# A decode block with its backward pass on one core: the last second-pass heads two by two, with 2 MiB gradient tiles

## The chip, the core and the metric

The kernel runs on one core of a Trainium2 chip. Its engines are TensorE (PE, with its weight loads shown as PEld), VectorE (DVE), ScalarE (ACT), GpSimd (POOL) and SyncE (SP, which here only issues transfers); 16 DMA engines move data between DRAM and the on-chip memory. The metric is the device time of one execution in microseconds, lower is better.

## The reference

One transformer decode block (two sequences, one new token each) and its vector-Jacobian product. What matters here is attention over a long cache and the gradients of that cache, which are as large as the cache itself.

```python
B, Sq, D = 2, 1, 640
Hq, Hkv, Sk, Dh = 32, 32, 4096, 128
...
q = (x @ wq).reshape(B, Sq, Hq, Dh)   # transposed to b h q d
scores = einsum("bhqd,bhkd->bhqk", q, k) * (Dh ** -0.5)
p = softmax(scores)
o = einsum("bhqk,bhkd->bhqd", p, v)
...
h  = x + A(layernorm(x), k_cache, v_cache, wq, wo)
h2 = h + B(layernorm(h), w1, w2)       # B: relu MLP, 640 -> 1728 -> 640
...
out, vjp = jax.vjp(f, x, k_cache, v_cache, wq, wo, w1, w2)
grads = vjp(grad_out)
```

For each of the 64 heads (2 sequences x 32) the gradients of the cache are outer products: gV = p times go (the gradient that reaches this head's output), and gK = ds times q, with ds = p * (V go - p.(V go)). Each is 4096 x 128 in bf16, 1 MiB. So 64 MiB of K and 64 MiB of V are read, 52 MiB of V are read a second time, and 128 MiB of gradients are written, beside some MiB of weights and weight gradients.

## The kernel before

The program records every engine's instructions in an order of its own, with generators that are advanced step by step; no scheduler moves them. A first pass (`p1_iter`) goes over all heads, reads K and V and makes scores, probabilities and outputs. A second pass (`p2_iter` and `p2_tail`) goes over the heads in the order `turns`, reads V again as tile `Wt` unless it was kept, and makes gV and gK. Between and beside them, background generators make the MLP, the weight gradients (`outer_rows`, tile `ot`, stored from ACT's queue) and the gradient of the input (`gx_gen`, which multiplies rows of wq on DVE, L669).

A head in the second pass lies as 128 partitions x 32 rows of 128, that is 8 KiB in a partition, both in DRAM and on chip (`natural`, L457). One head goes like this:

- POOL copies the head's probabilities twice beside each other (`pp`, L885); for some heads it also makes `pf` (L888).
- PE spreads the head's go and scaled q over all partitions into a PSUM bank (L878); ACT scales them by the head's softmax factor `rt` into `rb` (L883).
- V is transposed in four groups: four PE transposes into one of two PSUM banks (`t_ps`, L442), and an ACT copy out of it (`t_sb`, L447). Eight small matvecs per group (L455) then make `dp` = V go.
- DVE makes gV in two halves as an outer product of `rb` and `pp` (L843). In the last three heads ACT makes 4 of its 32 columns (L910). POOL issues the store (L911).
- In `p2_tail`, which runs inside the next head's steps, DVE makes ds (`gsp`, L854) and gK in two halves (L843), and POOL issues its store (L862).

Loads are issued by SP from one list (`queue`, emptied by `pump`) as long as a free tile of class `ld` is there. Large tiles of 8 KiB per partition are kept in classes: `ld` (loads), `g` (gradients), `f` (weight gradients), `q` (rows of wq, w2 and gq). `share` says how many tiles a class should own, and `give` hands a returned tile to a class that lacks one. When all of go is known (near the start of the last 20 heads) the space of wo is released, and a pool `big3` adds six tiles there: one `ld`, two `g`, three `q`. A tile is reused only after the transfer or the instructions that still use it have finished.

The main loop goes through `plan`, pairs of a first-pass and a second-pass index. In its late part it steps the second pass, `pump` and three background queues in turn.

Of the kernel before, what the change touches and what calls it, by code (L numbers as in the profile page):

```python
# [7 lines left out]
FP32 = mybir.dt.float32  # L8
BF16 = mybir.dt.bfloat16
# [6 lines left out]
def kernel(  # L16
# [20 lines left out]
    nc = tc.nc  # L37
# [41 lines left out]


    NBIG = 13
    homes = {"ld": list(range(NBIG)), "g": [], "f": [], "q": []}
    free = {tag: len(v) for tag, v in homes.items()}
    owned = dict(free)
    wanted = {}
# [11 lines left out]

    def goes_to(tag):

        if owned[tag] > wanted.get(tag, len(pools)):  # L100
            for other in homes:
                if owned[other] < wanted.get(other, 0):
                    return other
        return tag
# [329 lines left out]
    def pair_transpose(nat, g, dve=False, busy=0):  # L434
# [12 lines left out]
            nc.scalar.copy(out=t_sb[:], in_=t_ps[:])  # L447
        return t_sb

    def pair_matvec(dst, t_sb, g, vecs):  # L450
        v = t_sb[:].bitcast(BF16).rearrange("p j (k two) -> p j k two", two=2)
        for j in range(GT // 2):
            sc = g * GT + 2 * j
            for par in range(2):
                nc.tensor.matmul(dst[:, sc:sc + 2], lhsT=v[:, j, :, par], rhs=vecs[:, par, :],  # L455
                                 start=(par == 0), stop=(par == 1))
# [4 lines left out]
    def load_tile(what, i, tag):  # L461
        t = take(tag, [128, NSC, 128], what + "t")
        nc.sync.dma_start(out=t[:], in_=natural(A_k_cache if what == "K" else A_v_cache,
                                                *(turns if what == "W" else pairs)[i]))
        (S2 if what == "W" else S1).setdefault(i, {})[what] = t
        (S2 if what == "W" else S1)[i][what + "g"] = tag

    def p1_iter(i, dve_group, busy):

# [378 lines left out]
    def p2_tail(j):  # L848

        p = S2[j]  # L850
        bp, hp = turns[j]
        pair_matvec(p["dp"], p.pop("T3"), 3, gom[:, bp, hp, :, :])
        gsp = small.tile([128, NSC, 2], BF16, tag="gsp", bufs=2, name="gsp")
        nc.vector.scalar_tensor_tensor(  # L854
            out=gsp[:], in0=p["dp"][:, :, None].to_broadcast([128, NSC, 2]), scalar=negdot[:, hp, bp:bp + 1],
            in1=P_bf[:, p_slot[(bp, hp)], :, None].to_broadcast([128, NSC, 2]), op0=ALU.add, op1=ALU.mult)
        yield
        gK = take("g", [128, NSC, 128], "gK")
        outer_half(gK, p["rb"][:, 128:256], gsp, 0)
# [5 lines left out]
        yield  # L865

    NSB = 8

    def p2_iter(j, nsb):

        tail = p2_tail(j - 1) if j - 1 in S2 and "T3" in S2[j - 1] else iter(())
# [251 lines left out]
    while i <= NP1 + 1 or j <= NP1:  # L1123
        ii = i if i <= NP1 + 1 else None
        jj = j if i >= NP1 or (i >= P2_AT and (i - P2_AT) % 2 == 0) else None
        plan.append((ii, jj))
        i += 1
        if jj is not None:
            j += 1


    queue = []
# [3 lines left out]
    for n, (ii, jj) in enumerate(plan):  # L1136
        if ii is not None:
            if ii < NP1:
                queue.append(("K", ii))
        if ii is not None and ii >= 2:  # L1140
            queue.append(("V", ii - 2))
        ahead = plan[n + 1][1] if n + 1 < len(plan) and ii is not None else jj
        if ahead is not None and ahead < NP1 and turns[ahead] not in kept and ("W", ahead) not in queue:
            queue.append(("W", ahead))
        if ii in W_AT:
            queue.append(("w", W_AT.index(ii)))
        if ii in W2_AT:
            queue.append(("w2", W2_AT.index(ii)))
    def pump():
        while queue:  # L1150
            what, k = queue[0]
            if what == "w":
                load_weights(k)
            else:
                tag = "ld"
                if free["ld"] < 1:
                    return
                if what == "w2":
# [24 lines left out]
    for n, (i, j) in enumerate(plan):  # L1183
# [7 lines left out]
        if all_go and not late[0]:  # L1191
            wop.release()
            big3 = tc.alloc_tile_pool(name="big3", bufs=1, side="right")
            for tag in ("ld", "g", "g", "q", "q", "q"):
                more_home(tag, big3)
        late[0] = all_go
        more = int(late[0])
        if fin is not None and not bg2 and not bg3:
            share(ld=8 + 3 * more, g=7 + 3 * more)
        elif fin is not None and j >= H:  # L1200
            held = sum(bh in kept for bh in turns[j + 1:])
            share(ld=5 + held + more, g=5 + 2 * more, f=3, q=2 + 3 * more)
        while g2 is not None:
            p2_step()
        open_tail = [k for k in S2 if "T3" in S2[k]]
        if j is not None:
            if j < NP1:
                bg_until(("go", *turns[j]))
            nsb = 0 if i is not None else NSB if j < H and fin is None else NSB // 2 if j >= NP1 - 3 else 0
            g2 = p2_iter(j, nsb) if j < NP1 else p2_tail(NP1 - 1)  # L1210
# [20 lines left out]
        if i is None:  # L1231
            spread[0] = 2
            at_k[0] = 1
            k = 0
            while g2 is not None:
                p2_step()
                pump()
                slot[0] = int(k in ((1, 3, 5) if j <= H else (1, 4)))
# [69 lines left out]
```

## Time and profile before

| what | value |
|---|---|
| runs | 891.4, 893.67 (median), 894.74 us |
| profiled execution | 892.4 us, its span 890.6 us |
| DMA | 361.84 MB, mean 406 GB/s |
| busy | PE 83%, PEld 70%, DVE 77%, ACT 53%, POOL 23% |
| one gradient product (L843, 128 x 2048) | 1.22 us on DVE, 256 in all |
| gV store, issue to landing | 6.3 us least, 15.1 median, 35.7 most |
| gK store, issue to landing | 9.0 us least, 15.4 median, 35.9 most |
| last gK store issued | 874.91 us |

The page of the profile gives the busy time per engine, the span in 40 slices of 22.3 us with the share of the DMA engines and the rate, the DMA queues with packets and bytes, and the costliest groups of instructions by line. The trace also answers with busy time in any window, with an engine's instructions in order of time, and with who waited for whom. A transfer shows in two places: the instruction that issues it, and the packets on the 16 DMA engines, each of which carries a sixteenth of it.

### The profile page before, as it was taken

The page shows a single profiled execution, that of the slowest core. Times are in us where ns is not written, and L with a number is a line of the kernel's source. Part 1 is how long each engine was busy: PE and PEld are TensorE (multiplying, and loading weights), DVE is VectorE, ACT ScalarE, POOL GpSimd, SP SyncE. Part 2 cuts the span into 40 slices and gives each one's busy share as a digit, 9 for nine tenths or more (in the row PEclk, how much of TensorE's full clock was granted, in tenths as well). Part 3 has the DMA queues.
Part 4 walks back from the last instruction along what each step waited for, and adds up shares of the span by engine and source line. Part 5 has one row for each costly group of instructions (what it writes and reads, how often), then busy time and mean ns, then how long its engine had stood idle before and what let it go on. Part 6 is the DMA issues. An engine that isn't in the chain of part 4 may idle for free. (4 is left out here: it accounts for less than half of the span.)

```text
span 890.6 us, 24645 instructions
## 1 busy us (share of the span) xinstructions
PE 740.5 (83%) x10145; PEld 622.4 (70%) x10145; DVE 687.8 (77%) x1283; ACT 469.7 (53%) x1184; POOL 204.3 (23%) x342
## 2 busy tenths in 40 slices
PE   4999899999999998888888767885888888658871
PEld 4887788888887887777777656764666665536561
DVE  2665779876789897796796888786988467899992
ACT  1344334443455665454547766554567766437751
POOL 1344434342310000000023321121323011111141
PEclk9999989999999999997995555555557765555555
DMA  9999999999889999999999999999999999999995
GB/s 377 419 411 404 409 407 419 410 415 408 350 325 369 422 422 424 422 421 424 422 390 423 420 419 420 419 416 416 391 404 413 424 425 425 424 426 424 423 421 245
DMA packets 56304, 361.84 MB, mean 406 GB/s; under 512 B 5696, under 2 KB 11904, under 8 KB 15488
## 3 DMA queue, kind: packets, MB, share of 16 engines
q1 hardware_dynamic: 34536, 211.13, 58.1%
q0 software_dynamic: 18432, 134.23, 36.2%
q10 hardware_dynamic: 3224, 14.92, 4.1%
q8 instruction: 80, 1.31, 0.6%
q14 instruction: 32, 0.26, 0.1%
HBM read 211.11 MB, written 149.13 MB: 404 GB/s over the span
## 5 line engine op out<-in xcount | busy, mean ns | idle before, releaser
L447 ACT COPY t_sb<-t_ps 128x512 f32<-128x512 f32 x479 | 273.1, 587 | 186.3 <-PE t_ps L442 181.7
L455 PEld LDWEIGHTS <-t_sb 128*128 128x128 bf16 x4096 | 169.9, 103 | 83.7 <-ACT t_sb L447 42.3
L442 PE MATMUL t_ps<-ident_f,Wt 128*128 128x128 f32 x832 | 201.0, 393 | 0.4 <-ACT t_sb L447 0.4
L483 DVE TENSOR_TENSOR pk<-Kt,ep 128x2048 bf16<-128x2048 bf16 x128 | 156.2, 1221 | 44.7 <-ACT ep L534 24.9
L476 PE MATMUL m_ps<-pk,Vt 128*128 128x129 bf16 x2048 | 176.1, 223 | 13.3 <-DMA Vt<-in_A_v_cache_dram 12.6
L843 DVE TENSOR_TENSOR gK<-rb,gsp 128x2048 bf16<-128x2048 bf16 x128 | 153.8, 1226 | 28.0 <-DMA out_dram<-gV 26.2
L843 DVE TENSOR_TENSOR gV<-rb,pp 128x2048 bf16<-128x2048 bf16 (+2 forms) x128 | 147.1, 1172 | 30.8 <-DMA out_dram<-gK 24.0
L442 PEld LDWEIGHTS t_ps<-ident_f,Wt 128*128 128x128 f32 x832 | 140.4, 205 | 31.9 <-issue 25.0
L442 PE MATMUL t_ps<-ident_f,Kt 128*128 128x128 f32 x1024 | 154.7, 287 | 4.6 <-DMA Kt<-in_A_k_cache_dram 4.5
L476 PEld LDWEIGHTS <-Vt 128*128 128x128 bf16 x2048 | 131.0, 99 | 16.9 <-DMA Vt<-in_A_v_cache_dram 14.9
L442 PEld LDWEIGHTS t_ps<-ident_f,Kt 128*128 128x128 f32 x1024 | 117.0, 148 | 6.1 <-issue 3.4
L493 POOL COPY pk<-ep 128x16 bf16<-128x16 bf16 x80 | 83.1, 1041 | 151.3 <-ACT ep L534 112.7
L455 PE MATMUL dp_ps<-gom,t_sb 128*128 128x2 bf16 x2048 | 96.0, 168 | 23.3 <-ACT t_sb L447 22.9
L911 POOL DMA_DIRECT2D out_dram<-gV x64 | 34.3, 536 | 307.8 <-DVE nb L526 114.3
L455 PE MATMUL s_ps<-gom,t_sb 128*128 128x2 bf16 x2048 | 80.2, 164 | 1.2 <-DVE t_sb L445 1.2
L862 POOL DMA_DIRECT2D out_dram<-gK x64 | 34.1, 533 | 202.0 <-DVE gK L843 156.8
L593 ACT CAST MT<-m_ps 128x128 bf16<-128x128 f32 x64 | 17.1, 266 | 116.3 <-PE m_ps L476 116.3
L978 ACT CAST ot<-o_ps 128x512 bf16<-128x512 f32 (+3 forms) x152 | 67.0, 498 | 9.7 <-DMA out_dram<-ot 8.5
L883 ACT ACTIVATE rb<-dp_ps,rt 128x256 bf16<-128x256 f32 x64 | 30.2, 472 | 46.5 <-PE dp_ps L878 44.8
L669 DVE CUSTOM_DVE_ANT_0 rows<-wo_t,rows 128x640 bf16<-128x640 bf16 x64 | 52.3, 817 | 0.4 <-ACT rows L647 0.2
L669 DVE CUSTOM_DVE_ANT_0 rows<-wqs,gqr 128x1024 bf16<-128x1024 bf16 x40 | 48.8, 1219 | 0.2
L669 DVE CUSTOM_DVE_ANT_0 rows<-w_t,rows 128x640 bf16<-128x640 bf16 (+2 forms) x58 | 45.8, 790 | 1.2 <-ACT rows L647 0.5
(194 smaller groups left out, 720.4 us busy)
## 6 DMA issues: line engine op xcount, KB each, us to landing
Kt<-in_A_k_cache_dram SPq DMA_DIRECT2D x64, 1024.0 KB, 16.4
Vt<-in_A_v_cache_dram SPq DMA_DIRECT2D x64, 1024.0 KB, 16.6
out_dram<-gV POOLq DMA_DIRECT2D x64, 1024.0 KB, 15.1
out_dram<-gK POOLq DMA_DIRECT2D x64, 1024.0 KB, 15.4
Wt<-in_A_v_cache_dram SPq DMA_DIRECT2D x52, 1024.0 KB, 11.8
out_dram<-ot ACTq DMA_DIRECT2D x6, 960.0 KB, 12.4
wq_t<-in_A_wq_dram SPq DMA_DIRECT2D x5, 1024.0 KB, 11.0
wqs<-in_A_wq_dram SPq DMA_DIRECT2D x5, 1024.0 KB, 16.1
```

The costliest lines, as they stand in the source:

```text
L442: nc.tensor.transpose(t_ps[:, j, :], natf[:, 2 * cc:2 * cc + 2, :].rearrange("p c k -> p (c k)"), ident_f[:])
L447: nc.scalar.copy(out=t_sb[:], in_=t_ps[:])
L455: nc.tensor.matmul(dst[:, sc:sc + 2], lhsT=v[:, j, :, par], rhs=vecs[:, par, :], start=(par == 0), stop=(par == 1))
L476: nc.tensor.matmul(r["m"][:, 0:129], lhsT=r["V"][:, sc, :], rhs=r["pk"][sc // HALF][:, sc % HALF, 0:129], start=(sc == 0), stop=(sc == NSC ...
L483: nc.vector.tensor_tensor(out=p["pk"][k][:, :, 0:128].rearrange("p s (a two) -> p s a two", two=2), in0=p["K"][:, sl, :].rearrange("p s (a ...
L493: nc.gpsimd.tensor_copy(out=col, in_=e)
L669: nc.vector.tensor_tensor_reduce(out=junk[0:kc, 0:width], in0=in0, in1=in1, scale=1.0, scalar=0.0, op0=ALU.mult, op1=ALU.add, accum_out=acc)
L843: nc.vector.tensor_tensor(out=pairs_view(dst[:, sl, :]), in0=row.rearrange("p (a two) -> p a two", two=2)[:, None, :, :].to_broadcast([128 ...
L862: nc.gpsimd.dma_start(out=natural(out_2, bp, hp), in_=gK[:])
L883: nc.scalar.activation(out=rb[:], in_=bank[:, 128:384], func=ACT.Copy, scale=rt[:, b, h:h + 1])
L911: nc.gpsimd.dma_start(out=natural(out_3, b, h), in_=gV[:])
L978: nc.scalar.copy(out=ot[0:P, k, n0:n0 + nn], in_=o_ps[0:P, 0:nn])
```

## The change

The last 20 second-pass heads (second pass index 44 to 63, `PAIRS_AT` = 44) are made in ten pairs of neighbouring heads.

- A pair lies as 128 partitions x 64 rows: head h in partitions 0 to 63, head h + 1 in 64 to 127, 16 KiB in a partition (`pair_natural`). V is loaded in two tiles of 1 MiB, each half of every partition's rows (`load_half`).
- `both_iter` does for a pair what `p2_iter` does for a head, with eight transposed groups; each matvec has the go of both heads as its right side, and later steps take rows 0 to 63 from one and 64 to 127 from the other. `rb` is made for both heads at once, with a factor per partition that two POOL copies put together (`by_half`, into a free column of `Uc`); the probabilities of the pair are brought into its layout by four products with `sel` and two ACT copies into slots of `P_bf` that are no longer needed (`spare`).
- gV and gK of a pair are each one tile of class `gp`, 16 KiB per partition, made in four products and stored in one transfer of 2 MiB from POOL. The last pair stores each of its two tiles in two halves.
- ACT's share of gV in the last three heads is gone.
- `big3` holds three `gp` tiles in place of the six tiles of 8 KiB. The classes are shared anew: four `g` tiles stay in their class while the first pair is made, after it none; `ld` wants three more from the second pair on. When the background is done, `ld` wants all 16.

```diff
-    homes = {"ld": list(range(NBIG)), "g": [], "f": [], "q": []}
+    homes = {"ld": list(range(NBIG)), "g": [], "f": [], "q": [], "gp": []}
...
-        if owned[tag] > wanted.get(tag, len(pools)):
+        if tag != "gp" and owned[tag] > wanted.get(tag, len(pools)):
...
+    def both_matvec(dst, t_sb, g, vecs):
+        v = t_sb[:].bitcast(BF16).rearrange("p j (k two) -> p j k two", two=2)
+        for j in range(GT // 2):
+            sc = g * GT + 2 * j
+            for par in range(2):
+                nc.tensor.matmul(dst[:, :, sc:sc + 2], lhsT=v[:, j, :, par], rhs=vecs[:, :, par, :],
+                                 start=(par == 0), stop=(par == 1))
...
+    def pair_natural(cache, b, h):
+        return cache[b, h:h + 2].rearrange("h (p sc) d -> (h p) sc d", sc=2 * NSC)
+
+    def load_half(i, k, tag):
+        t = take(tag, [128, NSC, 128], "Wt")
+        nc.sync.dma_start(out=t[:], in_=pair_natural(A_v_cache, *turns[i])[:, k * NSC:(k + 1) * NSC, :])
+        S2.setdefault(i, {})[f"W{k}"] = t
...
+    def spare(k):
+
+        return P_bf[:, 2 + 4 * k:6 + 4 * k, :].rearrange("p a (s t) -> p (a s) t", t=2)
+
+    def by_half(dst, src, h):
+        for k in range(2):
+            rows = slice(64 * k, 64 * k + 64)
+            nc.gpsimd.tensor_copy(out=dst[rows], in_=src[rows, h + k:h + k + 1])
+
+    def both_tail(j):
+
+        p = S2[j]
+        bp, hp = turns[j]
+        both_matvec(p["dp"], p.pop("T7"), 7, gom[:, bp, hp:hp + 2, :, :])
+        gsp = spare(2)
+        for k in range(2):
+            rows = slice(64 * k, 64 * k + 64)
+            nc.vector.scalar_tensor_tensor(
+                out=gsp[rows], in0=p["dp"][rows, k, :, None].to_broadcast([64, 2 * NSC, 2]),
+                scalar=negdot[rows, hp + k, bp:bp + 1], in1=p["pp"][rows], op0=ALU.add, op1=ALU.mult)
+        yield
+        gK = take("gp", [128, 2 * NSC, 128], "gK")
+        dst = pair_natural(out_2, bp, hp)
+        for k in range(4):
+            outer_half(gK, p["rb"][:, 128:256], gsp, k)
+            if j == NP1 - 2 and k == 1:
+                nc.gpsimd.dma_start(out=dst[:, 0:NSC, :], in_=gK[:, 0:NSC, :])
+            if k < 3:
+                yield
+        if j == NP1 - 2:
+            nc.gpsimd.dma_start(out=dst[:, NSC:2 * NSC, :], in_=gK[:, NSC:2 * NSC, :])
+        else:
+            nc.gpsimd.dma_start(out=dst, in_=gK[:])
+        give(gK)
...
+    def both_iter(j):
+
+        tail = tail_of(j)
+        c = S2[j]
+        next(tail, None)
...
+        rts = Uc[:, 0, j // 2 % 2:j // 2 % 2 + 1]
+        by_half(rts, rt[:, b, :], h)
+        rb = mats.tile([128, 256], BF16, tag="rb", bufs=3, name="rb")
+        nc.scalar.activation(out=rb[:], in_=bank[:, 128:384], func=ACT.Copy, scale=rts)
+        pp = spare(j // 2 % 2)
+        for k in range(2):
+            rows = slice(64 * k, 64 * k + 64)
+            nc.scalar.copy(out=pp[rows].rearrange("p (q s) t -> p q s t", q=2),
+                           in_=pps[rows, k, :, :, None].to_broadcast([64, 2, NSC, 2]))
+        c.update(rb=rb, pp=pp)
+        c["T0"] = pair_transpose(c["W0"], 0)
+        next(tail, None)
+        yield
+        for _ in tail:
+            yield
+        gV = None
+        for g in range(1, 8):
+            W = c[f"W{g // 4}"]
+            c[f"T{g}"] = pair_transpose(W, g % 4)
+            if g % 4 == 3:
+                give(W)
+            both_matvec(c["dp"], c.pop(f"T{g - 1}"), g - 1, go)
+            if g >= 4:
+                if gV is None:
+                    gV = take("gp", [128, 2 * NSC, 128], "gV")
+                outer_half(gV, c["rb"][:, 0:128], c["pp"], g - 4)
...
+            nc.gpsimd.dma_start(out=pair_natural(out_3, b, h), in_=gV[:])
+        give(gV)
...
-            for tag in ("ld", "g", "g", "q", "q", "q"):
-                more_home(tag, big3)
+            for _ in range(3):
+                more_home("gp", big3)
...
-            share(ld=8 + 3 * more, g=7 + 3 * more)
+            share(ld=16)
...
-            share(ld=5 + held + more, g=5 + 2 * more, f=3, q=2 + 3 * more)
+            share(ld=5 + held + 3 * (j > PAIRS_AT), g=5 if not more else 4 * (j == PAIRS_AT), f=3, q=2 + 3 * more)
```

More of the change, by code (lines that the diff above doesn't have):

```diff
@@ L865, in p2_tail, with tail_of @@
         yield
+    def tail_of(j):
+        if j - 1 in S2 and "T3" in S2[j - 1]:
+            return p2_tail(j - 1)
+        if j - 2 in S2 and "T7" in S2[j - 2]:
+            return both_tail(j - 2)
+        return iter(())
+    def spare(k):
[4 more added lines that the diff above has]
+            nc.gpsimd.tensor_copy(out=dst[rows], in_=src[rows, h + k:h + k + 1])
@@ new lines, in both_tail @@
+    def both_tail(j):
[22 more added lines that the diff above has]
+        give(gK)
+        del S2[j]
+        yield
@@ new lines, in both_iter @@
+    def both_iter(j):
+        tail = tail_of(j)
+        c = S2[j]
+        next(tail, None)
+        b, h = turns[j]
+        go = gom[:, b, h:h + 2, :, :]
+        bank = pst([128, 512], FP32, "sps", "dp_ps")
+        for k, col in enumerate((goc, qsc)):
+            for q in range(2):
+                nc.tensor.matmul(bank[64 * q:64 * q + 64, 128 + k * 128:256 + k * 128],
+                                 lhsT=col[:, h + q, b:b + 1].to_broadcast([128, 64]), rhs=ident_bf[:],
+                                 start=True, stop=True)
+        pps = bank[:, 384:512].rearrange("p (k q s) -> p k q s", k=2, q=2)
+        for q in range(2):
+            for k in range(2):
+                nc.tensor.matmul(pps[:, k, q, :], lhsT=sel[:, q, :, :].rearrange("p c k -> p (c k)"),
+                                 rhs=P_bf[:, p_slot[(b, h + k)], :], start=True, stop=True)
+        c["dp"] = bank[:, 0:4 * NSC].rearrange("p (k s) -> p k s", k=2)
+        rts = Uc[:, 0, j // 2 % 2:j // 2 % 2 + 1]
[3 more added lines that the diff above has]
+        pp = spare(j // 2 % 2)
+        for k in range(2):
+            rows = slice(64 * k, 64 * k + 64)
[6 more added lines that the diff above has]
+        for _ in tail:
+            yield
+        gV = None
[9 more added lines that the diff above has]
+                outer_half(gV, c["rb"][:, 0:128], c["pp"], g - 4)
+                if j == NP1 - 2 and g == 5:
+                    nc.gpsimd.dma_start(out=pair_natural(out_3, b, h)[:, 0:NSC, :], in_=gV[:, 0:NSC, :])
+            yield
+        if j == NP1 - 2:
+            nc.gpsimd.dma_start(out=pair_natural(out_3, b, h)[:, NSC:2 * NSC, :], in_=gV[:, NSC:2 * NSC, :])
+        else:
+            nc.gpsimd.dma_start(out=pair_natural(out_3, b, h), in_=gV[:])
+        give(gV)
+        yield
+        yield
@@ L867 @@
     NSB = 8
+    PAIRS_AT = 2 * H - 2 * (H - 2 * KEPT[1]) // 2
     def p2_iter(j, nsb):
-        tail = p2_tail(j - 1) if j - 1 in S2 and "T3" in S2[j - 1] else iter(())
+        tail = tail_of(j)
         c = S2[j]
@@ L1128 @@
         if jj is not None:
-            j += 1
+            j += 2 if PAIRS_AT <= jj < NP1 else 1
     queue = []
@@ L1143 @@
         if ahead is not None and ahead < NP1 and turns[ahead] not in kept and ("W", ahead) not in queue:
-            queue.append(("W", ahead))
+            queue += [("X", (ahead, 0)), ("X", (ahead, 1))] if ahead >= PAIRS_AT else [("W", ahead)]
         if ii in W_AT:
@@ L1157, in pump @@
                     return
-                if what == "w2":
+                if what == "X":
+                    load_half(*k, tag)
+                elif what == "w2":
                     w2_tiles[k] = load_w2(k, tag)
@@ L1193 @@
             big3 = tc.alloc_tile_pool(name="big3", bufs=1, side="right")
-            for tag in ("ld", "g", "g", "q", "q", "q"):
-                more_home(tag, big3)
+            for _ in range(3):
+                more_home("gp", big3)
+            assert j == PAIRS_AT
         late[0] = all_go
@@ L1208 @@
                 bg_until(("go", *turns[j]))
+                assert j < PAIRS_AT or ("go", *turns[j + 1]) in done
             nsb = 0 if i is not None else NSB if j < H and fin is None else NSB // 2 if j >= NP1 - 3 else 0
-            g2 = p2_iter(j, nsb) if j < NP1 else p2_tail(NP1 - 1)
+            g2 = both_iter(j) if PAIRS_AT <= j < NP1 else p2_iter(j, nsb) if j < NP1 else both_tail(NP1 - 2)
         elif open_tail:
@@ L1237 @@
                 pump()
-                slot[0] = int(k in ((1, 3, 5) if j <= H else (1, 4)))
+                slot[0] = int((k if j < PAIRS_AT else k % 7) in ((1, 3, 5) if j <= H else (1, 4)))
                 k += 1
```

## The prediction

> **What bounds the kernel now.** I read the page's slices first, then its DMA queues, then busy time by stage, the waits, and last the end in steps of one or two us. The slices show 16 DMA engines busy at nine tenths or more almost throughout, the last slice apart.
>
> ```profile
> DMA  9999999999889999999999999999999999999995
> GB/s 377 419 411 404 409 407 419 410 415 408 350 325 369 422 422 424 422 421 424 422 390 423 420 419 420 419 416 416 391 404 413 424 425 425 424 426 424 423 421 245
> ...
> q1 hardware_dynamic: 34536, 211.13, 58.1%
> q0 software_dynamic: 18432, 134.23, 36.2%
> q10 hardware_dynamic: 3224, 14.92, 4.1%
> q8 instruction: 80, 1.31, 0.6%
> ```
>
> Queue q0 holds the gradient stores (packets, MB, share of 16 engines). In the slices from 690 us on, where the change acts, the rate stays at 421 to 426 GB/s.
>
> By POOL's stores the 20 changed heads begin near 700 us: the 20th gV store from the end is issued at 705.65, the last at 872.67. The windows from there (us, length, busy time of PE, PEld, DVE, ACT, POOL, clock, DMA share, GB/s):
>
> ```profile
> 700.00:750.00 50.00, 42.60 (x444) 32.07 (x444) 30.24 (x35) 34.42 (x73) 7.47 (x16) 0.64 1.01 426
> 750.00:800.00 50.00, 30.96 (x262) 22.41 (x260) 44.39 (x66) 22.15 (x51) 7.42 (x15) 0.53 1.01 425
> ...
> 860.00:870.00 10.00, 9.30 (x85) 7.72 (x84) 9.93 (x16) 7.01 (x17) 5.93 (x9) 0.50 1.00 416
> ```
>
> In each of them DMA has no gap. DVE is slack until 750 and full at the end, as PE is. The waits from 690 to 760 say what DVE's slack is:
>
> ```profile
> DVE gK L843 <- DMA out_dram<-gV: 13.1, 5, 4.6
> ...
> DVE gV L843 <- DMA out_dram<-gK: 11.0, 4, 3.0
> ```
>
> That is 24.1 us in which DVE waits for an older store to leave its tile. From 760 to 850 the same waits come to 4.1 us. So stores pace DVE first, and later both are full together. The end:
>
> ```profile
> 878.00:880.00 2.00, 0.00 (x0) 0.00 (x0) 0.00 (x0) 0.00 (x0) 0.00 (x0) 0.50 1.00 418
> 880.00:881.00 1.00, 0.00 (x0) 0.00 (x0) 0.00 (x0) 0.00 (x0) 0.00 (x0) 0.50 0.76 320
> 881.00:882.00 1.00, 0.00 (x0) 0.00 (x0) 0.00 (x0) 0.00 (x0) 0.00 (x0) 0.50 0.29 123
> 882.00:883.00 1.00, 0.00 (x0) 0.00 (x0) 0.00 (x0) 0.00 (x0) 0.00 (x0) 0.50 0.10 41
> 884.00:886.00 2.00, 0.00 (x0) 0.00 (x0) 0.00 (x0) 0.00 (x0) 0.00 (x0) 0.50 0.06 25
> 886.00:888.00 2.00, 0.00 (x0) 0.00 (x0) 0.00 (x0) 0.00 (x0) 0.00 (x0) 0.50 0.07 29
> ```
>
> No compute engine works after 876. A share of 0.06 is one engine of 16, and 25 GB/s is what one of them moves (424/16 = 26.5). So one DMA engine is about 7 us behind the rest, and that one sets the end. The last store is issued at 874.91; one store occupies an engine for 0.362 x 890.6 / 128 = 2.52 us (share of q0 over 128 stores), so the late engine takes up the last store near 886.4. The quickest store lands 6.3 us after its issue, so 3.8 us are latency. The last store could therefore have come 886.4 - 874.9 - 3.8 = 7.7 us later without moving the end. This slack carries the forecast.
>
> **The change, part by part.** The bytes are the same: 20 MiB of V read again, 40 MiB of gradients written.
>
> *Packets.* The 40 stores of 1 MiB with 8 KiB rows become 18 of 2 MiB with 16 KiB rows and 4 halves. Mean packets without the 16 small completion packets a transfer: q0 16384 of 8192 B in 0.362 x 890.6 x 16 = 5158 us, 314.8 ns each; q10 2900 of 5145 B in 584 us, 201 ns each. The line through both is 0.0372 ns per byte and 10 ns per packet. 5120 packets become 2560 (the four halves still move 8 KiB rows, a tenth, left out): 2560 x 10 ns / 16 engines = -1.6 us. The bound on the other side is q8, the only row with 16 KiB packets: 0.006 x 890.6 x 16 / 80 = 1.07 us each, against 0.62 by the line, which would be 2560 x 0.45 / 16 = +72 us. I take -1.6, because q8 carries instructions one packet at a time and q0 is the very path. If rows are cut at 8 KiB it is 0.
>
> *A rule weighed on the stores.* The DMA share is 1.00 to 1.02 while 1 MiB stores run, and a store's 2.52 us of engine time is hardly more than its bytes at 426 GB/s (2.46 us), so a fixed cost per store is at most 0.06 us: 18 fewer stores are worth 1.1 us.
> The Trainium skill, "DMA: Bandwidth & Descriptors", section "Anatomy of one DMA — SWDGE (gpsimd) path", fits about 2.0 us fixed per DMA plus the bytes. By that, as an estimate, 18 fewer stores would save 36 us. The trace disagrees, since the stores overlap.
>
> *DVE.* The outer products (L843, 1.22 us each) stay 8 for two heads. The last three heads lose ACT's help: their gV takes 2.36 instead of 2.08 us, +0.8 us. The gsp step (L854, 128x64, 0.278 us) becomes two of 64x128 for two heads. Bounds are 0 (same time) and 20 x 0.278 = +5.6 us (double). Small f32 operations of 10 columns take 0.17 us, so 54 more columns cost 0.108 us, 64 more 0.13: 20 x 0.13 = +2.6. In sum DVE gets +3.4 us. Its cover is the 7.7 us of slack of the late engine; without it the end moves by 3.4.
>
> *ACT.* Ten fewer rb (L883, 0.474) are -4.7 us, twelve fewer gV columns (L910, 0.39) -4.7, twenty pp copies of 64x128 out of PSUM (nearest: the 128x128 casts of L978 at 0.27) +5.4. ACT is 69% busy between 700 and 750: nothing.
>
> *PE.* Transposes and matvecs stay in number; each matvec has 4 columns instead of 2, behind weight loads as before. Four small products with sel per pair, at 0.16 (L455) to 0.27 us (L878), are 40 x 0.2 = 8 us over 180 us. PE has 7.4 us free of 50 between 700 and 750, 19 of 50 after, and runs short only from 855 on (2 pairs, 1.6 us, under the slack).
>
> *The new wait.* rb needs the per-head factors side by side, and two POOL copies make them. POOL is in order, and they stand behind the previous pair's gV store, which waits for DVE's last gV product. Behind rb on ACT queue two pp copies, the first eviction of the pair and the row evictions of the background work; PE gets two transposes further (two t_ps banks) and stands, and DVE's next gV waits for rb and pp. Price per pair from that product on: store issue 0.53, two copies at 0.23 to 1.31 (range of the pp copies, which shared DVE's hours), so 1.0 to 3.2 us, plus rb 0.47 and pp 0.54. It is covered while DVE makes gsp and four gK products (5.6 us). Value 0; without cover 2 to 4 us a pair.
>
> *Tiles and queues.* Seven 1 MiB gradient tiles (ten in the last heads) become three of 2 MiB; loads get 8 instead of 6, and four old tiles stay aside during the first pair. On SP the order is the old one but for one V load that moves ahead of a w2 load and the two wqs loads behind it: one MiB, 2.5 us later for those, needed only many us later. In the first pair DVE finds three fresh tiles and loses about 12.8 us of waits (3.04, 4.61, 2.65, 2.51 before four pieces between 700 and 722), but the DMA engines are full, so the next wait is the third or fourth 2 MiB tile. The stores get lumpier: gV can go near 706, gK only when PE has done eight groups (8.5 us of PE a head, so near 720). Stores issued before take 15.1 us median to land, hence an empty store queue of 0 to 5 us, which loads fill in part. I take +1.5 us, nearer the covered end because the late engine comes in with a backlog.
>
> *Sum.* 892.4 (own time of the profiled execution; span 890.6) - 1.6 + 1.5 = 892.3. The median of the runs shown is 1.3 us higher, so 893.6.
>
> **The rivals.**
> - *No change to speak of* (forecast, 0.42): 893.6, own range 889 to 898.
> - *Stores starve* (0.20), slower. Three tiles hold at most 4 MiB in flight while the third is filled, and the lumps come once a pair. For: DVE needs 10 us a head with the row work between 750 and 850, so a tile takes about 10 us to fill. Against: loads fill the gaps until about 820. It decides once the late engine's 7.7 us are used up: a gap of 5 us on three of the first pairs and 5 at the end, less 7.7, is +12: 906.
> - *The POOL wait shows* (0.16), slower. For: DVE and PE are both over 90% after 855, and PE is at 9.0 of 10 us between 740 and 750. Against: gK products cover it. If 1 us a pair stays over ten pairs less what slack DVE's 3.4 leaves (4.3), +6: 899.
> - *The late engine catches up* (0.20), faster. The bytes after 880 are 0.6 MB, 1.5 us if spread evenly: the end would come near 881.5 instead of 888.9. With the packets that is -9, at best 884.7; half of it 889. For: the lag is not in the bytes, since every store is split over all engines alike, and it is not constant (stores land 6.3 to 35.7 us after issue). Against: nothing in the change alters the split.
> The Trainium skill, same page, section "Queues, rings and completion order", says that an engine goes round its queues packet by packet; by that 16 KiB stores beside 8 KiB loads would get two thirds of an engine instead of half. No row of this trace shows it.
> - *Fixed costs per store, or rows cut up or slow* (0.02): down to -68 us (18 x 3.8) or up to +72; the full engines speak against the first.
>
> **How the numbers follow.** Faster by over 0.5% (4.5 us, about what a measurement of this kernel can tell from no change): 0.21, the late engine and half the last case. Within: 0.42. Slower: 0.37. The 8-in-10 range reaches from the late engine caught up to the starving stores, 885 to 906; what lies beyond is under 0.2.
>
> **What will show it.** Right: DMA share 1.0 and over 420 GB/s from 700 to 880, 16 KiB store packets near 0.62 us, one engine alone at the end. Wrong: windows with DMA share under 0.97 after 700 (starving), ACT's rb waiting on POOL for more than 1 us a pair with PE idle behind it, packets near 1 us, or an end in which all engines stop together.

## The result and the profile after

| | before | after |
|---|---|---|
| runs side by side | 893.95 us (891.4 to 894.84) | 905.9 us (903.24 to 906.1) |
| ratio | | 1.0132, 95% interval 1.0114 to 1.0151 |
| profiled execution, its span | 892.4, 890.6 us | 904.8, 903.0 us |
| last store issued | 874.91 us | 892.61 us |
| last byte stored | 888.50 us | 897.36 us |

The change costs 12 us, 1.3%. The forecast, no change, was wrong. First the page of the changed kernel: rate in the 40 slices (22.6 us each) and the store queue and load queue.

```profile
DMA  9999999999989999999999999999999999899886
GB/s 377 420 410 405 410 408 420 409 414 407 342 346 367 423 422 425 420 425 423 391 378 422 419 418 415 420 417 420 387 422 415 420 425 419 332 425 425 359 350 279
...
q1 hardware_dynamic: 34536, 211.13, 57.8%
q0 software_dynamic: 15840, 134.22, 35.7%
```

The bytes are the old ones. The rate is about the old one as well, up to a hole from 768 us on (332) and a slack stretch from 835 us on (359, 350, 279), where the kernel before ran at 424. The busy time by stage says who left the holes (columns as in the prediction):

```profile
700.00:750.00 50.00, 40.95 (x439) 32.04 (x437) 23.50 (x24) 32.86 (x69) 3.38 (x9) 0.67 1.01 423
750.00:760.00 10.00, 1.53 (x31) 1.02 (x32) 4.07 (x6) 0.00 (x0) 0.00 (x0) 0.50 1.01 423
...
770.00:780.00 10.00, 10.00 (x81) 7.79 (x81) 9.97 (x12) 5.39 (x14) 0.53 (x1) 0.50 0.72 287
...
830.00:860.00 30.00, 24.77 (x207) 16.65 (x206) 29.80 (x39) 19.41 (x40) 3.21 (x6) 0.61 0.89 367
860.00:880.00 20.00, 15.22 (x163) 12.52 (x162) 19.55 (x34) 9.24 (x21) 5.61 (x8) 0.59 0.86 356
...
897.00:898.00 1.00, 0.00 (x0) 0.00 (x0) 0.00 (x0) 0.00 (x0) 0.00 (x0) 0.50 0.02 8
898.00:903.00 5.00, 0.00 (x0) 0.00 (x0) 0.00 (x0) 0.00 (x0) 0.00 (x0) 0.50 0.00 0
```

Read it downwards. Until 760 the DMA engines are full, but DVE does 23.5 us of work between 700 and 750 where it did 30.2 before, and then 4.07 of 10. After that DVE is full (9.97 of 10, 29.8 of 30, 19.55 of 20) and the DMA engines have gaps. DVE lost work early, while transfers hid it, and cannot make it up later. In the last lines all DMA engines stop together, near 897.4; the late engine of the kernel before is gone, and five us follow in which nothing moves. DVE's waits from 690 to 760 (us in total, times, longest):

```profile
DVE rows L685 <- DMA wqs<-in_A_wq_dram: 16.8, 1, 16.8
DVE gK L859 <- DMA out_dram<-gK: 6.1, 1, 6.1
...
DVE gV L859 <- DMA out_dram<-gK: 3.7, 1, 3.7
```

The waits for old stores, 24.1 us before, are down to 9.8. In their place stands one wait of 16.8 us, from 739.07 to 755.90, for the first `wqs` tile, the weights of a background row product that stands in DVE's order between two pieces of a gV. The stores behind it wait too: one is issued at 734.39, the next at 763.25. The `wqs` loads after and before:

```profile
L1142 SPq DMA_DIRECT2D wqs<-in_A_wq_dram x5: 327/336/862, 721.0 to 815.2; - x5
...
DMA to landing us min/median/max: 17.6/26.3/34.9
```

```profile
L1025 SPq DMA_DIRECT2D wqs<-in_A_wq_dram x5: 328/337/1057, 711.4 to 803.7; - x5
...
DMA to landing us min/median/max: 10.6/16.1/21.6
```

The first of them, the slowest in both, is issued 720.97 - 711.41 = 9.6 us later and takes 34.9 - 21.6 = 13.3 us more. Before, it landed at 733.0, 6.2 us ahead of its use at 739.2. So 9.6 + 13.3 - 6.2 = 16.7 us of waiting, against 16.8 measured.

To the end of the span it adds up thus: the last store is issued 17.7 us later; from there to the last byte 4.8 us pass instead of 13.6; from the last byte to the end of the span 5.7 instead of 2.1. 17.7 - 8.8 + 3.5 = 12.4 us, the difference of the two spans.

The 17.7 us are DVE's. From 690 us to the end of its last product, before and after:

```profile
690.00:874.61 184.61, 142.71 (x1306) 105.20 (x1303) 150.65 (x206) 111.02 (x237) 34.31 (x64) 0.56 1.01 424
```

```profile
690.00:892.31 202.31, 143.87 (x1363) 106.81 (x1361) 154.17 (x207) 109.29 (x238) 25.79 (x44) 0.58 0.95 395
```

It works 154.2 us instead of 150.7 and stands idle 48.1 us instead of 34.0.

### The profile page after: what moved, and what is told of

The parts are those of the page before. It is cut to its first block, busy times and chain, and to the rows that moved or that the text cites. A ratio compares the mean times of both kernels' runs of the same rounds, so it can differ in the third digit from the quotient of the medians.

```text
span 903.0 us, 24659 instructions
## 1 busy us (share of the span) xinstructions
PE 735.7 (81%) x10185; PEld 617.7 (68%) x10185; DVE 690.8 (76%) x1283; ACT 465.7 (52%) x1182; POOL 195.7 (22%) x321
## 5 line engine op out<-in xcount | busy, mean ns | idle before, releaser
L463 PEld LDWEIGHTS <-t_sb 128*128 128x128 bf16 x3456 | 137.7, 101 | 64.0 <-ACT t_sb L447 31.0
L442 PEld LDWEIGHTS t_ps<-ident_f,Wt 128*128 128x128 f32 x832 | 137.1, 201 | 28.2 <-issue 24.2
L442 PE MATMUL t_ps<-ident_f,Kt 128*128 128x128 f32 x1024 | 150.8, 282 | 3.7 <-DMA Kt<-in_A_k_cache_dram 3.7
L859 DVE TENSOR_TENSOR gK<-rb,gsp 128x2048 bf16<-128x2048 bf16 x88 | 105.7, 1226 | 22.2 <-DMA out_dram<-gV 11.5
L859 DVE TENSOR_TENSOR gV<-rb,pp 128x2048 bf16<-128x2048 bf16 x88 | 100.2, 1159 | 14.6 <-DMA out_dram<-gK 12.1
L463 PE MATMUL dp_ps<-gom,t_sb 128*128 128x2 bf16 x1408 | 65.2, 167 | 16.2 <-ACT t_sb L447 16.0
L1028 POOL DMA_DIRECT2D out_dram<-gV x44 | 23.5, 535 | 232.3 <-DVE nb L542 115.1
L1095 ACT CAST ot<-o_ps 128x512 bf16<-128x512 f32 (+3 forms) x152 | 66.9, 495 | 11.9 <-DMA out_dram<-ot 9.5
L685 DVE CUSTOM_DVE_ANT_0 rows<-wqs,gqr 128x1024 bf16<-128x1024 bf16 x40 | 48.8, 1220 | 17.2 <-DMA wqs<-in_A_wq_dram 16.8
L878 POOL DMA_DIRECT2D out_dram<-gK x44 | 23.4, 532 | 140.5 <-DVE gK L859 110.4
L859 DVE TENSOR_TENSOR gV<-rb,P_bf 128x2048 bf16<-128x2048 bf16 x40 | 47.3, 1218 | 3.7 <-DMA out_dram<-gK 3.7
L859 DVE TENSOR_TENSOR gK<-rb,P_bf 128x2048 bf16<-128x2048 bf16 x40 | 46.9, 1220 | 0.3
## 6 DMA issues: line engine op xcount, KB each, us to landing
out_dram<-gK POOLq DMA_DIRECT2D x46, 1024.0 KB, 13.3
```

The source lines that it names most:

```text
L442: nc.tensor.transpose(t_ps[:, j, :], natf[:, 2 * cc:2 * cc + 2, :].rearrange("p c k -> p (c k)"), ident_f[:])
L685: nc.vector.tensor_tensor_reduce(out=junk[0:kc, 0:width], in0=in0, in1=in1, scale=1.0, scalar=0.0, op0=ALU.mult, op1=ALU.add, accum_out=acc)
L859: nc.vector.tensor_tensor(out=pairs_view(dst[:, sl, :]), in0=row.rearrange("p (a two) -> p a two", two=2)[:, None, :, :].to_broadcast([128 ...
L1095: nc.scalar.copy(out=ot[0:P, k, n0:n0 + nn], in_=o_ps[0:P, 0:nn])
```

## The experiments

Ratios are to the kernel before, run on the same chip beside each kernel, with 95% intervals.

**Is it where the row product stands?** Three kernels leave the 16 KiB rows alone and help the `wqs` tile. `e_hold` holds V loads back until two `wqs` loads are issued:

```diff
+                if what == "X" and k[0] >= PAIRS_AT + 8 and fetched[0] < 2:
+                    return
```

> The changed kernel, but V loads of the pair at 52 and later are held back until the first two wqs loads are issued (two MiB move behind them). Late-row theory: DVE's wait of 16.8 us for wqs falls under 5 us, the last store is issued over 10 us earlier, and the time comes to 893 to 898. Starving-stores theory (three 2 MiB tiles cannot feed the DMA engines): the wait may go, but the time stays within 3 us of 905.9. POOL-wait theory (rb behind POOL's copies): 904 to 907.

904.67 us, 1.0136 (1.0121 to 1.0151): a miss of the late-row theory. The wait for `wqs` fell to 12.0 us in two stretches, not under 5, and other waits grew. `e_late` lets the first row product come 34 steps after its load instead of 16:

```diff
-            while c >= len(tiles) or (step[0] < tiles[c][1] + 16 and not forced[0]):
+            while c >= len(tiles) or (step[0] < tiles[c][1] + (34 if c == 0 else 16) and not forced[0]):
```

> The changed kernel, but DVE's first wqs row product is placed 34 steps after its load instead of 16; no load moves before it. Late-row theory: DVE no longer waits for wqs (under 3 us) and makes gradients in that time; 892 to 899. Starving-stores and POOL-wait theories: 904 to 907.

909.79 us, 1.0189 (1.0163 to 1.0215): a miss again. No wait for `wqs` is left, and between 690 and 850 DVE shows this one:

```profile
DVE P_bf L907 <- PE dp_ps L455: 28.3, 5, 16.5
```

That is `dp`, which needs V: now the V tiles are late. `e_wq_actq` issues the `wqs` loads from ACT, past the V loads:

```diff
-                nc.sync.dma_start(out=t[:], in_=wq_r[:, len(tiles), :])
+                nc.scalar.dma_start(out=t[:], in_=wq_r[:, len(tiles), :])
```

> The changed kernel with all its 16 KiB rows, but the five wqs loads are issued by ACT, so they go by the queue q10 and not behind the V loads in q1. Packet theory, where a queue's share of an engine goes by turns: with two load queues the loads have two turns of three, 8 + 8 KiB beside 16, so half the bytes again, and the wqs tile passes the V loads: landing 8 to 14 us after issue instead of 26, DVE's wait for it under 5 us, 896 to 902 (ACT's own waits for a free tile can cost up to 3 us). If the loads' lateness isn't what costs: 904 to 907.

904.32 us, 1.0136 (1.0121 to 1.0151): a miss in the time, though the landing fell to 14.0 to 23.9 us and the wait for `wqs` to nothing. DVE's waits from 700 to 830:

```profile
DVE P_bf L907 <- PE dp_ps L455: 16.8, 4, 7.3
DVE ml L752 <- PE mlp_ps L748: 14.1, 3, 7.4
```

`dp` needs V, and `mlp_ps` needs a weight tile of the same load queue. Loads as a whole are late; giving one of them the way makes another late.

**Why are loads late? The queues' shares.** The transfers between 735 and 745 us, in the order before, after, and `e_8kfull` (below); packets, MB, share of 16 engines:

```profile
q0 software_dynamic: 266, 1.95, 46.5%
q1 hardware_dynamic: 271, 1.96, 46.5%
```

```profile
q0 software_dynamic: 190, 2.83, 66.9%
q1 hardware_dynamic: 193, 1.38, 32.8%
```

```profile
q0 software_dynamic: 291, 2.12, 50.2%
q1 hardware_dynamic: 292, 2.09, 49.9%
```

Stores and loads move the same number of packets in each. A packet is one row of a transfer, so with 16 KiB rows on one side and rows of 7.5 or 8 on the other the bytes go two to one. In `e_wq_actq`, the `wqs` loads are a second load queue (q10; 735 to 745 us), and it is the same again by threes:

```profile
q0 software_dynamic: 150, 2.20, 51.3%
q10 hardware_dynamic: 146, 1.04, 24.9%
q1 hardware_dynamic: 144, 1.02, 24.1%
```

This fits that kernel's being no faster: q1, with V and the other weights, fell from a third to a quarter.

**The large tiles with 8 KiB rows.** `e_rows8k` cuts each 2 MiB store in two along the rows. Each half is then stored as soon as its products are done, so `e_8kfull` issues the second half first, and neither goes before the tile is full (gV in the same way):

```diff
-            nc.gpsimd.dma_start(out=dst, in_=gK[:])
+            nc.gpsimd.dma_start(out=dst[:, NSC:2 * NSC, :], in_=gK[:, NSC:2 * NSC, :])
+            nc.gpsimd.dma_start(out=dst[:, 0:NSC, :], in_=gK[:, 0:NSC, :])
```

> The changed kernel, but each 2 MiB store is issued as two of 1 MiB with 8 KiB rows, both when the tile is full; tiles, order and waits stay. If 16 KiB packets take two thirds of an engine beside 8 KiB loads and so hold up the wqs loads: loads get back to half of the rate between 710 and 745, DVE's wait for wqs falls from 16.8 to 8 us or less, 896 to 902. If only the place of the wqs loads in SP's order counts: the wait stays at 15 to 18 us and the time at 905 to 908 (packets cost 1 us more).

> As in the run with 1 MiB stores of 8 KiB rows, but the second half of each 2 MiB tile is stored first, so that in POOL's order neither half can go before the whole tile is full. What this run keeps of the change: tiles, lumps, order, waits; what it takes away: only the 16 KiB rows. Packet theory (16 KiB packets beside 8 KiB ones take two thirds of each engine, loads come late): loads get half again (200 to 215 GB/s beside stores), DVE waits under 2 us for wqs, 896 to 900 us. Theory of the early half (the earlier run with 8 KiB rows was fast because half of each tile left some us before the other): 902 to 906, with loads at half all the same.

897.43 us, 1.0043 (1.0025 to 1.006), and 898.03 us, 1.0054 (1.0034 to 1.0073). The early half makes no difference; the rows make 8 us of the 12. How the 8 us divide between loads in time and a shorter end, the later runs show. DVE's wait in `e_8kfull`:

```profile
DVE rows L685 <- DMA wqs<-in_A_wq_dram: 2.5, 1, 2.5
```

`wqs` is issued as late as in the changed kernel (721.9), lands in 25.3 us at most instead of 34.9, and that is almost in time. DVE gains far less than these 14.3 us: its waits for old stores go from 9.8 to 23.7 us, and its whole stand, from 690 us to its last product, only from 48.1 to 44.9. A wait of 16.8 us was not a loss of 16.8 us.

**The rule without the change.** `e_b4k` is the kernel before, with the V loads of the last 16 heads and the `wqs` loads cut to 4 KiB rows, the `wqs` loads like this:

```diff
+                for r in (slice(0, HD // 2), slice(HD // 2, HD)):
+                    nc.sync.dma_start(out=t[:, r], in_=wq_r[:, len(tiles), r])
```

> The kernel before, with 1 MiB tiles and 8 KiB store rows untouched, but its V loads of the last 16 heads and its wqs loads are cut in two, with 4 KiB rows instead of 8. Packet theory: loads beside stores get a third (about 140 GB/s against 280) with no 2 MiB tile anywhere, loads land as late as in the changed kernel, DVE waits for wqs or V for 8 us or more: 897 to 905, of which at most 1.5 us are the 2000 more packets at 10 ns. If the large tiles and lumps make the loads late and not the packets' sizes: loads stay at half, 892.5 to 895.

897.95 us, 1.0062 (1.0048 to 1.0077), with no large tile in it. Queues from 735 to 750 us:

```profile
q0 software_dynamic: 558, 4.06, 64.6%
q1 hardware_dynamic: 554, 2.27, 36.8%
```

DVE waits 9.5 us for `wqs` and 28.8 us for `dp` between 690 and 850. Late loads alone are worth 4 to 5.6 us here (5.6 less the 1.7 us of 2688 more packets, 21 MiB cut from 8 to 4 KiB rows, at the prediction's estimate of 10 ns over 16 engines).

`e_bdelay` delays the `wqs` loads of the kernel before by 17 steps and puts the first row product right behind:

```diff
+        hold[0] = step[0] + 17
...
+            if step[0] < hold[0]:
+                return
```

> The kernel before, but the wqs loads are issued 17 steps later, and DVE's first row product stands right behind the first of them, so that DVE waits for it some 10 to 17 us; nothing of the change is in it. Late-row theory: the wait less the 7.7 us of slack shows, 897 to 904. If the loss came from the large tiles or from POOL's wait: under 897.

892.97 us, 1.0 (0.9989 to 1.0012), with a wait for `wqs` of 8.0 us: a miss of the late-row theory as it was put. The waits for old stores fell from 28.2 to 22.4 us between 690 and 850, and the last store came 1.3 us later, which the slack at the end took. One late tile of 8 us was free here, while finished tiles were queued for storing; in the changed kernel 16.8 us used that queue up (q0 moved nothing from 755 to 760 us).

**Early or late pairs?** `e_8kfirst` stores only the first three pairs with 8 KiB rows (`elif j < PAIRS_AT + 6:` before the two halves), `e_8klast` only the others.

> The changed kernel, but the stores of its first three pairs (44, 46 and 48, those that run beside the V loads up to about 770 us) go as two of 1 MiB with 8 KiB rows, both when the tile is full; the later pairs keep 16 KiB rows. Packet theory (16 KiB rows do harm only while loads share the engines with them): 897 to 901, and the wait of DVE for the first wqs tile under 4 us. If 16 KiB rows cost something on their own wherever they are, in proportion to the stores: 903 to 904 (6 of 18 stores mended, 2.6 of 8 us).

> The mirror: 16 KiB rows in the first three pairs, two stores of 8 KiB rows in the later ones. Packet theory: the loads of 700 to 745 us are as late as in the changed kernel, DVE waits 12 us or more for the first wqs tile, 903 to 906. If 16 KiB rows cost in proportion wherever they are: 900 to 901.

897.12 us, 1.005 (1.0036 to 1.0064): three of ten pairs bring it all. DVE's first wait for `wqs` is 4.4 us, as against 17.9 in `e_8klast`; two more follow, so that the three come to 12.7. `e_8klast`, 901.42 us, 1.0105 (1.0087 to 1.0122), was a miss too: lower than the theory of late loads allowed. Cutting stores anywhere does something else besides; that is the question of the end, below. The two ran on one chip and differ by 4.3 us: so much more do the long rows cost early than late.

**The POOL wait.** `e_rows8k_act` and `e_act` make the two copies in front of `rb` on ACT, with 8 and 16 KiB rows:

```diff
-            nc.gpsimd.tensor_copy(out=dst[rows], in_=src[rows, h + k:h + k + 1])
+            nc.scalar.copy(out=dst[rows], in_=src[rows, h + k:h + k + 1])
```

> 1 MiB stores of 8 KiB rows, and the two factor copies before rb on ACT instead of POOL. The 8 KiB rows alone left 3.5 us over the kernel before. If that rest is the POOL wait (rb behind two copies behind a store that waits for DVE): the ACT wait of rb for POOL (34.7 us in three stretches) is gone and the time is 893 to 895. If the rest is the tiles' size (a tile comes free 2 MiB at a time) or DVE's added steps: the wait is gone too, and the time stays at 896 to 898.

> The changed kernel (16 KiB rows) with the two factor copies on ACT instead of POOL, nothing else. If the POOL wait is worth 3.5 us and adds to the late loads: 901 to 903. If the late load is the only thing on the path: DVE still stands some 16 us before the first wqs row product, 904 to 906.5. If the POOL wait were the main cause: 893 to 897.

894.02 us, 1.0011 (0.9996 to 1.0027), against 897.4 and 898.0 with POOL: 3 to 4 us. With 16 KiB rows 904.44 us, 1.0121 (1.0101 to 1.0141): not to be told from 905.9. `rb`'s wait for POOL between 760 and 850 in the changed kernel and in `e_8kfull`:

```profile
ACT rb L949 <- POOL Uc L897: 30.4, 4, 19.4
```

```profile
ACT rb L950 <- POOL Uc L897: 18.1, 3, 8.9
```

The longest wait of the first, 19.4 us up to 765.43, follows from DVE's own stand: POOL's gV store in front of the copies waits for DVE until 763.25. `e_8kfirst_act` combines 8 KiB rows in three pairs with copies on ACT.

> 8 KiB rows in the first three pairs only, and the factor copies on ACT; the later pairs keep 16 KiB rows. If the two causes found so far add as they did with 8 KiB rows everywhere: 897.1 less 3 to 4 = 893 to 894.5, level with the kernel before. If 16 KiB rows of the later pairs cost something that the POOL wait has hidden: 896 or more.

896.11 us, 1.0038 (1.0026 to 1.0051): a miss by 2 us, with all waits for POOL and `wqs` gone.

**The four old tiles.** `e_g0` gives them up at the first pair (`g=5 if not more else 0` in `share`).

> The changed kernel, but the four old 1 MiB gradient tiles are given up at the first pair instead of after it. Theory that the four old tiles kept aside starve the first pair or hold up the loads: wqs is issued 3 us or more earlier, DVE waits 10 us or less before it, 899 to 903. Packet theory: the loads beside 16 KiB stores are as slow as before, 904 to 907.

906.02 us, 1.0143 (1.0122 to 1.0164): nothing. The wait for `wqs` fell to 8.2 us, as the theory of the tiles had it, but `wqs` was issued no earlier (722.0), and a single wait for an old gK store of 20.2 us took its place.

**The end.** From the last byte to the end of POOL's closing drain, in the profiled executions: 4.9 to 5.4 us in the six kernels with 16 KiB rows in all pairs, 0.8 to 1.4 in the others. The first kind had moved 990 packets of q0 per engine, the second 1044 to 1152. In the second kind POOL stands before its 114th store, the one that takes them past 1024: that store starts 2.9 to 3.3 us after its gradient product is done, where 0.3 us is usual. Three kernels cut one, three and four of the late stores in two:

> The changed kernel with one more store of its 18 cut in two (gK of pair 56, far behind the loads in question). In the kernels with all 18 stores of 16 KiB rows POOL comes to the closing barrier 4.9 us after the last byte, in all with 6 or more of them cut 0.8 to 1.4 us. Theory of the count: it goes by how many packets q0 has moved per engine, 990 in the changed kernel (15840/16), 1044 where the first six stores are cut, with 1024 between: this run has 999, so the late POOL stays, 904 to 906.5. Theory of the pattern (all tiles alike to the end): one cut is enough, the gap falls to 1.4 and the time to 901 to 902.5.

> As before it with three stores cut (gV and gK of pair 56, gK of pair 58): 1017 packets of q0 per engine. Theory of the count with its step at 1024: the gap stays at 4.9 us, 903.5 to 906.5. If the number of stores decides (113 here, 110 in the changed kernel, 116 where the gap was short) the step may lie on either side.

> Four stores cut (gV and gK of pairs 56 and 58): 1026 packets per engine. Theory of the count with its step at 1024: the gap falls to about 1.4 us and the time by 3.5, 901 to 902.5, while the first wqs tile is as late as in the changed kernel (DVE waits 12 us or more).

905.03 us, 1.0143 (1.0129 to 1.0156); 904.26 us, 1.0136 (1.012 to 1.0153); 903.58 us, 1.0115 (1.0095 to 1.0135). The gaps are 5.0, 5.1 and 0.8 us, just as the count says (999, 1017 and 1026), but the time hardly moves. The last store of `e_split4` on POOL (start, length, the idle time before it):

```profile
898.68 0.54 POOL L920 DMA_DIRECT2D out_dram<-gK  x1 [4.32 <-issue]
```

DVE's last product was done at 895.81, 2.9 us earlier: the stand has only moved ahead of the last store. In the kernel before the same store comes early:

```profile
830.42 0.54 POOL L862 DMA_DIRECT2D out_dram<-gK  x1 [6.53 <-issue]
```

Its product, too, was done 2.9 us before. There other stores were in flight, and it shows in no wait of DVE. In `e_8kfirst_act` it stands at 882.29, third from the end, and in `e_rows8k_act` at 840.23; that goes with the 2 us between them, but was not tried by itself, and `e_8kfirst`, where it stands as late (884.78), is no slower than `e_8kfull` (840.36). Two kernels should pass the count far from the end, by cutting early gV stores by partitions, in two (18 heads) and in four (40 heads):

```diff
+        step_p = 128 // 4 if 4 <= j < 44 else 128
+        for p0 in range(0, 128, step_p):
+            nc.gpsimd.dma_start(out=natural(out_3, b, h)[p0:p0 + step_p], in_=gV[p0:p0 + step_p])
```

> The changed kernel with all its 16 KiB rows, but 18 early gV stores (heads 10 to 27, long before the change acts) are cut by partitions into two of 512 KiB each. That makes 128 stores by GpSimd, as many as in the kernel before, with rows of 8 KiB, and 1008 packets of q0 per engine (990 + 18 completion packets). If GpSimd's 4 us of its own come after 113 stores, whatever their size: they come near 840 us, the gap at the close is 1.4 us, 901 to 903. If they come after 1024 packets per engine: the gap stays at 4.9 us, 904 to 906.5.

> As before it, with the gV stores of heads 4 to 43 cut in four by partitions: 230 stores and 990 + 120 = 1110 packets per engine, of which the 1024th comes some 9 pair stores before the end, near 820 us. Theory of the packets: the stretch of 4 us of GpSimd moves there, away from the close, the gap at the close falls to about 1.1 us, and the time by up to 3.6 us, 902 to 903.5; the wait for the first wqs tile stays. If it goes by stores: 113 are reached before 600 us and 226 near the end, gap anywhere. If the closing gap has nothing to do with that count: 4.9 us and 904.5 to 907.

932.77 us, 1.0444 (1.0412 to 1.0476), and 956.2 us, 1.0716 (1.0688 to 1.0743). No theory gave such numbers: the cut stores themselves are slow (last section). `e_part2` with 128 stores and 1008 packets keeps a gap of 5.8 us, so it isn't the number of stores. `e_part4` has 1110 packets, but its 221st store, which passes 1024 at 890.03, starts 0.3 us after its product like any other, and the gap at the close is 4.9 us. So it isn't this count either. Without the small completion packets, of which a cut by partitions makes more, the count is 880 per engine in the changed kernel, in `e_part2` and in `e_part4`; 888, 904 and 912 with one, three and four stores cut; and 928 or more in the rest. A step between 904 and 912 fits every kernel here, but that was seen afterwards and no run tried it. What POOL does in that time stays open.

## Why the prediction was wrong

- **The step that failed** is the sentence on SP's queue, that one V load moves ahead of the `wqs` loads: "one MiB, 2.5 us later for those, needed only many us later". They were issued 9.6 us later and took 13.3 us more to land, with 6.2 us to spare. The order was as foretold. What made the issue late is that SP waited 3.5 us for an older gV store and 3.5 us for an older gK store to leave the tiles of a V load ahead of them and of the first `wqs` load, as it did not before (2.8 and 4.0 us in `e_8kfull`, so the longer rows are not the reason). What made the landing late is the rate at which that queue is served, which was taken as unchanged.
- That rate was in the text, as the rule of the Trainium skill, "DMA: Bandwidth & Descriptors", section "Queues, rings and completion order", that an engine goes round its queues packet by packet; but it stood beside the rival of the late engine, and no term of the sum was drawn from it. The changed kernel agrees with it: 190 packets to 193, 66.9% to 32.8%. The same section of the Trainium skill counts about 9 to 17 descriptors to a packet; here one turn is one packet of the trace, which is one row. By the packets' records from 735 to 745 us, a load packet starts in the last 6 ns of a store packet in 168 of 173 cases, another store packet in 15.
- That no row of the old trace shows the rule was a misreading. In the kernel before, from 808 to 832 us, weight gradients with 4 KiB rows (q10) go beside stores and loads with 8 KiB rows:

```profile
q0 software_dynamic: 555, 4.03, 39.9%
q1 hardware_dynamic: 545, 4.00, 39.5%
q10 hardware_dynamic: 553, 2.13, 21.7%
```

- **Sizes.** With 8 KiB rows 7 to 8 us of the 12 are gone, by ratios 0.8% to 0.9%. Late loads are about 4 of them: 4.3 between the medians of `e_8kfirst` and `e_8klast`, which both end with a short close, 2.5 between their last bytes in the profiled executions (893.8 and 896.3). The close is 3.5 in the profiled executions, and it was no term of the sum at all. The copies on ACT take 3 to 4 more. With both the kernel stands at 894.0, and the interval to the kernel before holds 1. No kernel here beats the one before.
- **The new wait** was valued at 0 and bounded by 2 to 4 us a pair without cover. It cost 3 to 4 us over all pairs once loads were in time: right in mechanism, mis-sized. The cover named, DVE's gsp and gK products, was short: in `e_8kfull` `rb` still waited 18.1 us for POOL between 760 and 850.
- **The slack** that carried the forecast, 7.7 us, was there. In `e_rows8k_act` the last store is issued 10.8 us later than in the kernel before, and the span is only 2.1 us longer. In the changed kernel the last store came 17.7 us later, more than any slack.
- **Packets.** By the packets' records (medians) one of 16 KiB of q0 takes 611 ns, two of 8 KiB 618: 2304 x 7 / 16 = -1.0 us against -1.6. Right.
- **DVE.** The two gsp pieces of a pair take 0.73 us, those of two heads 0.56: 10 x 0.17 = +1.7 against +2.6. In all DVE works 3.5 us more, against +3.4: right. The gsp pieces, the 2 MiB tiles and the lumps together cost no more than 2.4 us, net of what the late engine gave (upper end of `e_rows8k_act`).
- **The late engine caught up**, as that rival said: all stop together. Its 7 us did not come off the end, because the last store came 17.7 us later.
- **Stores starve** gave 906, the measured number, by another mechanism: the agreement is chance. The holes it foretold are there (0.72, 0.89, 0.86), but they follow DVE's stand. `e_8kfull`, with the same tiles and lumps, has holes too (0.80 from 830 to 860) and is 8 us faster.
- **The four old tiles** were counted with the +1.5 us for the first pair; `e_g0` shows them to be worth nothing.

## What to carry to other kernels

Before the rows of a transfer are made longer, look at what shares the engines with it: turns go by packets, so a longer row on one side takes bandwidth from the other, and full DMA engines do not show it. A stretch of the old profile in which transfers with unlike rows already run side by side gives the shares beforehand. Ask then which load is used soonest after it lands, and what stands behind its consumer in that engine's order; moving that consumer or that load alone only hands the wait on. And where transfers pace a kernel, finished tiles in flight are the reserve: a stand of 8 us was free, one of 17 was not, and of a wait that goes part comes back as a wait for old stores.

## What the runs showed of the hardware

- Queues take turns by packets of one row: 266 to 271, 190 to 193, 558 to 554, and 150 to 146 to 144 for three queues, with rows of 8, 16 and 4 KiB. A second load queue gave loads more of the engines: 49% instead of 33%.
- GpSimd stands once before a store, which starts 2.9 to 3.3 us after its product where 0.3 is usual: the 114th store, in each of the ten kernels that have 114 or more stores of whole tiles or of halves by rows. In the kernels with fewer, and in the two with gV cut by partitions, 4.9 to 5.8 us pass from the last byte to the end of its closing drain instead of 0.8 to 1.4.
- A store of 64 partitions is slower than one of 128 with the same rows: with 18 heads' gV cut so, the rate from 450 to 550 us was 358 GB/s instead of 411 in the changed kernel, with the DMA engines busy all the time in both; a tenth of q0's 8 KiB packets took 619 ns or more, where 309 is usual.
